# Moving the w_out sums on VectorE: behind the last square of chunk 0 instead of behind the second batch's K transpose

## The chip, the cores and the metric

The kernel runs on one core of one Trainium2 chip. The metric is the device time of one execution in microseconds (us). A profile of one execution comes with each kernel; its time axis starts at the first instruction, and its span is about 1.8 us shorter than the device time. The traced execution of a kernel is one of its timed runs, and every run has its mean granted TensorE clock beside its time (1.000 is full speed), so one can see whether a trace is typical.

## The reference, cut to what matters

```python
# attention with projected keys and values (8 batches, 8 heads, 1024 tokens, head size 64), then a feed-forward
k_proj = einsum('ks,bhsd->bhkd', E, k); v_proj = einsum('ks,bhsd->bhkd', F, v)
attn = softmax(q @ k_proj.T / sqrt(64));  x = attn @ v_proj        # x: 8192 x 512
h = maximum(x @ w_in, 0.0)                                         # w_in: 512 x 2048
out = (h * h) @ w_out                                              # w_out: 2048 x 512
```

## The kernel before

TensorE is the engine to keep busy. Each batch is cut into two chunks of 512 tokens. For a chunk, the first layer makes 16 blocks; ScalarE takes the relu of each and VectorE squares it. The second layer is then done in one of two ways. Chunk 0 of batch 0 uses plain products (L481). All later chunks use seven half-size products instead of eight, Strassen's scheme (L414), which needs sums of parts of `w_out` (`w_sum`, computed once) and of the squares (`h_sum`, computed per chunk).

```python
def sum_w_out(behind):
    with tc.issue_after(behind.queued.ins):     # these come later on VectorE than that instruction
        sum_w_out_now()

def sum_w_out_now():
    for j in range(2):
        ...
        up, down = w_out_sb[j], w_out_sb[j + 2]     # w_out arrives in four pieces
        b11, b12, b21, b22 = ...
        for o, x, y in ((t1, b12, b11), (t3, b22, b12), (t2, b22, t1), (t4, b21, t2)):
            nc.vector.tensor_tensor(out=o, in0=x, in1=y, op=ALU.subtract)      # L150, eight in all
```

The attention of the next chunk or batch is put between the steps of the feed-forward. `at(n, f)` traces `f` after step `n`. For batch 0, steps 1 to 16 are the first layer of chunk 0, 17 to 32 its second layer, 33 to 48 the first layer of chunk 1, and 49 on its seven products:

```python
at(21, att.transpose_q_chunk, 1, Q0, 0); at(21, att.transpose_q_chunk, 1, Q0, 1)  # PE, then VectorE copies qT (L269)
at(23, att.chunk_scores, 1, 0);          at(23, att.chunk_scores, 1, 1)           # PE, needs qT; ScalarE exp
at(25, att.sums, 0)                      # softmax sums: PE, three ScalarE passes, four VectorE copies of rs (L334)
at(27, att.chunk_values, 1, 0); ...      # values: PE, VectorE multiplies into xT (L375), which chunk 1 reads
...
at(39, nxt.transpose_k)                  # second batch; the old anchor of sum_w_out
at(45, nxt.sums, 0)
at(48, nxt.values, 0, True)              # True: its PSUM comes from the four banks that the products also use
at(46, sum_w_out, nxt)
```

Only TensorE's order is given by hand. On the other engines the scheduler chooses the order at compile time. In the profile lines, `ps_bank` and `ps_att` are the banks of PSUM, the memory that the matmuls of this kernel write; here a product can start only when one of its banks has been read out.

The softmax here doesn't subtract the row's maximum and nothing guards it: scores larger than these inputs give would overflow.

Of the kernel before, what the change touches and what calls it, by code (L numbers as in the profile page):

```python
# [12 lines left out]
ALU = mybir.AluOpType  # L13
# [5 lines left out]
def kernel(  # L19
# [11 lines left out]
    nc = tc.nc  # L31
# [21 lines left out]
    HF, HM = NFB // 2, DM // 2  # L53
# [19 lines left out]
    def bank(shape=(P, 512), dtype=F32):  # L73
        return fps.tile(list(shape), dtype, tag="bank", name="ps_bank")
# [91 lines left out]
    def projection(name, e_bf):  # L166
        ps = bank([P, NI, KP], BF16)
        view = e_bf[:].rearrange("k (p i) -> k i p", i=NI)
        for i in range(NI):
            nc.tensor.transpose(ps[:, i, :], view[:, i, :], ident[0:KP, 0:KP])  # L170
        t = const_pool.tile([P, NI, KP], BF16, name=name)
        nc.vector.tensor_copy(t[:], ps[:])
        return t

    def warm(n):

        ps = bank()
        for _ in range(n):
            nc.tensor.matmul(ps[:], lhsT=zeros[:, 0:P], rhs=zeros[:], start=True, stop=True)  # L179
# [5 lines left out]
    class Attention:  # L185
# [58 lines left out]
        def transpose_k(self, gs=(0, 1)):  # L244
            ps = bank([P, H // 2, 2, KP], BF16)
            rows = slice((LO, HI)[gs[0]].start, (LO, HI)[gs[-1]].stop)
            g = slice(gs[0], gs[-1] + 1)
            for j in range(H // 2):
                nc.tensor.transpose(
                    ps[:, j, g, :].rearrange("p g k -> p (g k)"),  # L250
                    self.kp[rows, j].rearrange("k a d -> k (a d)"), ident[rows, rows]
                )
            self.queued = nc.vector.tensor_copy(self.kT[:, :, g], ps[:, :, g])

        def transpose_k_dma(self):
            nc.sync.dma_start_transpose(
# [122 lines left out]
    class Ffn:  # L379
# [6 lines left out]
        def square(self, c, fb, ps):  # L386
            r = relu_pool.tile([P, TCH], BF16, name="h_relu")
            nc.scalar.activation(r[:], ps[:], AF.Relu)  # L388
            rv = r.rearrange("p (a t) -> p a t", a=2)
            nc.vector.tensor_tensor(out=self.hsq[c][:, fb // HF, :, fb % HF, :], in0=rv, in1=rv, op=ALU.mult)  # L390

        def quarter(self, c, kh, a):
            return self.hsq[c][:, kh, a]
# [153 lines left out]
    with tc.manual_schedule(engines={PE}):  # L547
        e_bf = soft_pool.tile([KP, S], BF16, tag="expT", name="e_bf")
        nc.vector.tensor_copy(e_bf[:], e_f32[:])
        nc.scalar.copy(K0[:, 0:2], k_f32[:])  # L550
        warm(8)
        ET = projection("ET", e_bf)
        warm(4)
        att = Attention(0)
        att.project_k(0)
        warm(1)
        att.transpose_q_chunk(0, Q0, 0)
        att.transpose_k((0,))
        warm(3)
        att.chunk_scores(0, 0)  # L560
        FT = projection("FT", f_bf)
        warm(3)
        att.project_k(1)
        att.chunk_sums(0, 0)
        att.transpose_q_chunk(0, Q0, 1)
        att.transpose_k((1,))
        warm(2)
        att.chunk_scores(0, 1)
        warm(2)
        att.project_v(V_PIECES[0])  # L570
        warm(1)
        att.chunk_sums(0, 1)
        att.chunk_values(0, 0)
        warm(2)

        coming = None
        for b in range(B):
            plan = {}

            def at(step, fn, *args, **kwargs):  # L580
                plan.setdefault(step, []).append(lambda: fn(*args, **kwargs))

            if b == 0:
                at(1, att.project_v, V_PIECES[1])
                at(2, att.chunk_values, 0, 1, (0,))
                at(2, att.project_v, V_PIECES[2])
                at(3, att.chunk_values, 0, 1, (1,))
                at(21, att.transpose_q_chunk, 1, Q0, 0)
                at(21, att.transpose_q_chunk, 1, Q0, 1)
                at(23, att.chunk_scores, 1, 0)  # L590
                at(23, att.chunk_scores, 1, 1)
                at(25, att.sums, 0)
                at(27, att.chunk_values, 1, 0)
                at(27, att.chunk_values, 1, 1)
                nxt = Attention(1)
                nxt.load()
            if b + 1 < B:
                if b + 2 < B:
                    coming = Attention(b + 2)
                    coming.load()  # L600
                if b == 0:
                    at(36, nxt.project)
                    at(39, nxt.transpose_q, 0)
                    at(39, nxt.transpose_q, 1)
                    at(39, nxt.transpose_k)
                    at(41, nxt.scores, 0)
                    at(41, nxt.scores, 1)
                    at(44, nxt.transpose_q, 2)
                    at(44, nxt.transpose_q, 3)
                    at(45, nxt.sums, 0)  # L610
                    at(48, nxt.values, 0, True)
                    at(48, nxt.scores, 2)
                    at(46, sum_w_out, nxt)
                    at(51, nxt.values, 1)
                    at(51, nxt.scores, 3)
                    at(55, nxt.sums, 2)
                    at(55, nxt.values, 2)
                    at(57, nxt.values, 3)
                else:
                    at(12, nxt.scores, 0)  # L620
                    at(12, nxt.scores, 1)
                    at(16, nxt.sums, 0)
                    at(16, nxt.values, 0)
                    at(20, nxt.scores, 2)
                    at(26, nxt.values, 1)
                    at(26, nxt.scores, 3)
                    at(46, nxt.sums, 2)
                    at(46, nxt.values, 2)
                    at(50, nxt.values, 3)
                if b + 2 < B:  # L630
                    if b == 0:
                        at(59, coming.project)
                        at(61, coming.transpose_q_dma)
                        at(62, coming.transpose_k)
                    else:
                        at(26, coming.project)
                        at(30, coming.transpose_q_dma)
                        at(28, coming.transpose_k_dma)
            for step, _ in enumerate(Ffn(att, b == 0).steps(), 1):
                for stage in plan.pop(step, []):  # L640
                    stage()
            assert not plan, plan
            att, nxt = nxt, coming
# [30 lines left out]
```

## Time and profile before

| | before |
|---|---|
| time, median of the first three runs | 499.49 us (498.38 to 499.56) |
| TensorE busy | 97% of the span |
| largest wait of TensorE after 30 us | 3.65 us, at 75.0 us |
| clock after it | 0.50 for 3.4 us |
| VectorE idle ahead of the chunk-1 softmax | 3.71 us and 5.95 us |

The page of the profile, kernel before (part 1: busy us, share of the span, instructions):

```profile
PE 482.8 (97%) x3446; PEld 293.4 (59%) x3482; DVE 310.9 (62%) x596; ACT 281.6 (57%) x426; POOL 32.5 (7%) x45
```

The timeline of TensorE, kernel before. The columns are start us, length us, engine, line, operation, output<-inputs, shape, count, and in brackets the idle time before it and what ended it:

```profile
37.53 4.48 PE L481 MATMUL ps_bank<-w_out,hsq 128*128 128x512 bf16 x20
...
42.74 1.89 PE L481 MATMUL ps_bank<-w_out,hsq 128*128 128x512 bf16 x8
...
54.19 3.87 PE L475 MATMUL ps_bank<-xT,w_in 128*128 128x512 bf16 x16
...
74.07 0.94 PE L414 MATMUL ps_bank<-w_out,hsq 128*128 128x256 bf16 x7
78.65 1.67 PE L414 MATMUL ps_bank<-w_out,hsq 128*128 128x256 bf16 x9 [3.65 <-DVE hsq L390]
...
96.95 10.52 PE L475 MATMUL ps_bank<-xT,w_in 128*128 128x512 bf16 x47
```

The reader should see one hole, at 75.0 us: the first of the seven products waits for a square (L390). The *start* is the first second-layer matmul of chunk 0 (37.53). **Stretch A** runs from the start to the first first-layer matmul of chunk 1 (54.19): 16.66 us. **Stretch B** runs from there to the first first-layer matmul of the third batch (96.95): 42.76 us.

The reason why the square is late is in the timeline of VectorE, kernel before:

```profile
42.49 1.29 DVE L269 COPY qT<-ps_bank 128x1024 bf16<-128x1024 bf16 x2 [3.71 <-PE ps_bank L265]
49.73 2.80 DVE L334 COPY rs<-rs 32x1024 f32<-32x1024 f32 x4 [5.95 <-ACT rs L329]
...
74.06 0.68 DVE L150 TENSOR_TENSOR w_sum<-w_out,w_out 128x1024 bf16<-128x1024 bf16 x1
74.75 2.78 DVE L334 COPY rs<-rs 32x1024 f32<-32x1024 f32 x4
77.56 0.69 DVE L150 TENSOR_TENSOR w_sum<-w_out,w_sum 128x1024 bf16<-128x1024 bf16 x1
78.17 0.42 DVE L390 TENSOR_TENSOR hsq<-h_relu 128x512 bf16<-128x512 bf16 x1
```

VectorE has no gap over 0.2 us from 59.98 to 84 us. The square's relu was done at 74.0 us, but two w_sum subtractions and four copies stand before it. Earlier, VectorE was idle for 3.71 and 5.95 us.

The clock, by narrow windows of the same trace (stretch, its length, busy us of TensorE, its weight loads, VectorE, ScalarE and GpSimd, then the granted TensorE clock; the last two columns, on DMA, are not used here):

```profile
78.00:79.00 1.00, 0.35 (x4) 0.32 (x5) 1.00 (x3) 0.00 (x0) 0.00 (x0) 1.00 1.25 209
79.50:80.00 0.50, 0.50 (x4) 0.37 (x3) 0.50 (x2) 0.00 (x0) 0.00 (x0) 0.50 1.24 205
83.00:84.00 1.00, 1.00 (x11) 0.90 (x10) 1.00 (x3) 0.94 (x1) 0.00 (x0) 1.00 1.25 209
```

### The profile page before, as it was taken

To read this page: it belongs to the slowest core of one execution; us is meant where nothing else is said; L and a number is where in the kernel's file an instruction comes from. 1 tells how busy PE (TensorE), PEld (TensorE's weight loads), DVE (VectorE), ACT (ScalarE), POOL (GpSimd) and SP (SyncE) were. 2 spreads that over 40 slices of the span, in tenths; PEclk is the share of its full clock that TensorE was granted. 3 is DMA by queue.
4 is the path that set the end of the run, shared out by engine and by line. 5 is a ranking of instruction groups with operands and counts; after the bars stand their busy time and mean duration, and the time that the engine had idled before them with its cause. 6 is when DMAs were issued, how large, how long until landed. Compare 5 with 4: busy or idle time off the path is not lost.

```text
span 497.8 us, 8559 instructions
## 1 busy us (share of the span) xinstructions
PE 482.8 (97%) x3446; PEld 293.4 (59%) x3482; DVE 310.9 (62%) x596; ACT 281.6 (57%) x426; POOL 32.5 (7%) x45
## 2 busy tenths in 40 slices
PE   7899997999999999999999999999999999999996
PEld 3444454647566574847557475665648475666755
DVE  2351797767584766757585675838566674847271
ACT  2464473476564846567573856558474665645451
POOL 7430100100100010000100000000000000000000
PEclk8999998999999999999999999999999999999999
DMA  9999999995992069710994016020611102020202
GB/s 172 204 205 213 237 208 207 218 179 113 201 196 85 1 120 196 144 59 1 190 212 119 0 53 129 3 84 1 123 58 47 40 2 85 1 86 0 86 1 86
DMA packets 75416, 54.30 MB, mean 109 GB/s; under 512 B 29168, under 2 KB 74480, under 8 KB 75376
## 3 DMA queue, kind: packets, MB, share of 16 engines
q0 software_dynamic: 30640, 29.23, 36.2%
q1 hardware_dynamic: 44736, 24.52, 19.6%
q8 instruction: 27, 0.44, 0.3%
q14 instruction: 13, 0.11, 0.1%
HBM read 59.24 MB, written 16.78 MB: 153 GB/s over the span
## 4 chain that ended last, share of the span: by engine, by line
PE 89%; DVE 6%; ACT 2%; issue 1%; DMA 1%; DVEq 0%; POOLq 0%
PE ps_bank L475 42%; PE ps_bank L414 37%; PE ps_bank L219 2%; PE ps_att L346 2%; PE ps_att L290 2%; DMA K_sb<-in_k_dram 1%; DVE rs L334 1%; PE ps_bank L481 1%; DVE xT L375 1%; PE ps_att L324 1%; DVE w_sum L150 1%; DVE hsq L390 1%; PE ps_bank L228 1%; PE ps_bank L179 1%; DVE qT L279 1%
## 5 line engine op out<-in xcount | busy, mean ns | idle before, releaser
L475 PE MATMUL ps_bank<-xT,w_in 128*128 128x512 bf16 x992 | 223.3, 379 | 3.0 <-DVE xT L375 1.1
L388 ACT ACTIVATE h_relu<-ps_bank 128x512 bf16<-128x512 f32 x256 | 151.1, 600 | 90.4 <-PE ps_bank L475 90.1
L475 PEld LDWEIGHTS <-w_in 128*128 128x128 bf16 x1024 | 99.2, 98 | 120.4 <-issue 6.2
L390 DVE TENSOR_TENSOR hsq<-h_relu 128x512 bf16<-128x512 bf16 x256 | 105.9, 423 | 84.3 <-ACT h_relu L388 83.0
L414 PEld LDWEIGHTS <-hsq 128*128 128x128 bf16 x960 | 92.1, 98 | 22.1 <-issue 6.9
L414 PEld LDWEIGHTS <-h_sum 128*128 128x128 bf16 x720 | 69.8, 98 | 12.4 <-issue 4.1
L414 PE MATMUL ps_bank<-w_out,hsq 128*128 128x256 bf16 x480 | 60.6, 274 | 3.6 <-DVE hsq L390 3.6
L414 PE MATMUL ps_bank<-w_sum,h_sum 128*128 128x256 bf16 x480 | 57.9, 275 | 0.0
L414 PE MATMUL ps_bank<-w_sum,hsq 128*128 128x256 bf16 x480 | 57.5, 272 | 0.3 <-ACT u L432 0.3
L424 DVE TENSOR_TENSOR o_sb<-ps_bank,u 128x512 f32<-128x512 f32 x30 | 20.7, 691 | 55.9 <-PE ps_bank L414 30.9
L334 DVE COPY rs<-rs 32x1024 f32<-32x1024 f32 x60 | 41.1, 685 | 11.7 <-ACT rs L329 10.6
L432 ACT COPY u<-ps_bank 128x512 f32<-128x512 f32 x30 | 17.5, 585 | 54.5 <-PE ps_bank L414 54.5
L304 ACT ACTIVATE expT<-ps_att 128x1024 bf16<-128x1024 f32 x32 | 31.9, 1025 | 6.6 <-PE ps_att L290 6.6
L350 DVE TENSOR_TENSOR xT<-ps_att,rs 128x512 bf16<-128x512 f32 x54 | 34.1, 685 | 0.4
L414 PE MATMUL ps_bank<-w_out,h_sum 128*128 128x256 bf16 x240 | 28.6, 273 | 0.5 <-DVE o_sb L424 0.5
L422 ACT COPY o_sb<-ps_bank 128x512 f32<-128x512 f32 x30 | 17.6, 585 | 17.7 <-PE ps_bank L414 17.6
L402 DVE TENSOR_TENSOR h_sum<-hsq 128x1024 bf16<-128x1024 bf16 x30 | 20.7, 691 | 1.0
L402 DVE TENSOR_TENSOR h_sum<-h_sum,hsq 128x1024 bf16<-128x1024 bf16 x30 | 20.6, 688 | 0.5
L402 DVE TENSOR_TENSOR hsq<-hsq 128x1024 bf16<-128x1024 bf16 x30 | 20.5, 685 | 0.0
L402 DVE TENSOR_TENSOR h_sum<-hsq,h_sum 128x1024 bf16<-128x1024 bf16 x30 | 20.5, 684 | 0.0
L80 POOL DMA_DIRECT2D K_sb<-in_k_dram x9 | 7.8, 861 | 138.5 <-PE ps_bank L220 134.1
L330 ACT ACTIVATE rs<-rs 128x1024 f32<-128x1024 f32 x15 | 15.9, 1062 | 0.5
(71 smaller groups left out, 251.0 us busy)
## 6 DMA issues: line engine op xcount, KB each, us to landing
out_dram<-o_sb SPq DMA_DIRECT2D x64, 256.0 KB, 2.3
K_sb<-in_k_dram POOLq DMA_DIRECT2D x7, 1024.0 KB, 13.7
V_sb<-in_v_dram POOLq DMA_DIRECT2D x7, 1024.0 KB, 19.7
Q_sb<-in_q_dram POOLq DMA_DIRECT2D x7, 1024.0 KB, 15.9
w_out<-in_moe_w_out_dram POOLq DMA_DIRECT2D x4, 512.0 KB, 17.8
w_in<-in_moe_w_in_dram POOLq DMA_DIRECT2D x3, 512.0 KB, 14.7
k_f<-in_k_dram SPq DMA_DIRECT2D x1, 512.0 KB, 4.3
Q_sb<-in_q_dram POOLq DMA_DIRECT2D x2, 256.0 KB, 8.1
```

The source lines that it names most:

```text
L304: nc.scalar.activation(e[:], ps[:], AF.Exp, scale=SCALE)
L330: nc.scalar.activation(rs[1][:], rs[1][:], AF.Exp, scale=-1.0)
L334: nc.vector.tensor_copy(rs[j][lack:lack + 32], rs[j][have:have + 32])
L350: nc.vector.tensor_tensor(out=self.xT[:, pr, :, par], in0=ps_x[par].rearrange("p (c t) -> p c t", c=2), in1=rs[:, par].rearrange("p (c t) ...
L388: nc.scalar.activation(r[:], ps[:], AF.Relu)
L390: nc.vector.tensor_tensor(out=self.hsq[c][:, fb // HF, :, fb % HF, :], in0=rv, in1=rv, op=ALU.mult)
L402: nc.vector.tensor_tensor(out=o, in0=x, in1=y, op=op)
L414: nc.tensor.matmul(ps[:, i * HM:(i + 1) * HM], lhsT=h[:, fb, i * P:(i + 1) * P], rhs=w_out_form(n, fb), start=fresh and i == 0 and fb == 0 ...
L422: nc.scalar.copy(o[:], ps[:])
L424: nc.vector.tensor_tensor(out=o[:], in0=ps[:], in1=more[:], op=ALU.add)
L432: nc.scalar.copy(u[:], ps[:])
L475: nc.tensor.matmul(ps[:], lhsT=w_in_blk(cb, fb), rhs=self.xT[:, cb, c].rearrange("p a t -> p (a t)"), start=(cb == 0), stop=(cb == NCB - 1),)
```

## The change

The intent is to take the eight subtractions (8 x 0.60 us = 4.8 us) out of the full stretch and put them into VectorE's idle time before chunk 1. The anchor becomes the last square of batch 0, chunk 0.

```diff
-            self.queued = nc.vector.tensor_copy(self.kT[:, :, g], ps[:, :, g])
+            nc.vector.tensor_copy(self.kT[:, :, g], ps[:, :, g])
 ...  # in Ffn.square
-            nc.vector.tensor_tensor(out=self.hsq[c][:, fb // HF, :, fb % HF, :], in0=rv, in1=rv, op=ALU.mult)
+            self.queued = nc.vector.tensor_tensor(out=self.hsq[c][:, fb // HF, :, fb % HF, :], in0=rv, in1=rv, op=ALU.mult)
 ...
             plan = {}
+            ffn = Ffn(att, b == 0)
 ...
-                    at(46, sum_w_out, nxt)
+                    at(18, sum_w_out, ffn)
 ...
-            for step, _ in enumerate(Ffn(att, b == 0).steps(), 1):
+            for step, _ in enumerate(ffn.steps(), 1):
```

## The prediction

> **What bounds the kernel.** By the page of the profile, TensorE is busy 97% of the 497.8 us span and carries 89% of the chain that ended last; VectorE is busy 62%. The exception is batch 0, chunk 1: the timeline shows VectorE back to back from 59.98 to about 84.3 us: squares, softmax copies, half sums and the eight w_sum subtractions (65.1 to 78.5 us, about 0.60 us each). The chain that ended last runs there through VectorE. TensorE's one large wait there is 3.65 us, 75.0 to 78.65 us, for the square of L390. In narrow windows the granted clock is 1.00 until 79, 0.50 from about 79.2 to 82.5, and 1.00 again; 17 second-layer matmuls take 3.40 us there, 16 elsewhere about 1.75. The Trainium skill ("TensorE: Matmul & The Clock Gate", Part 1) says the clock halves after an idle window of about 3.4 us and returns after a busy one; this trace agrees (3.3 us at half clock, 1.65 us lost). So the hole costs about 5.3 us.
>
> **What the change does.** No work is added. The eight subtractions, 8 x 0.6 = 4.8 us, may start behind the last square of chunk 0, which ends at 38.8 us; VectorE is then idle 3.7 us until 42.49 us and 5.95 us before 49.73 us. I expect them at about 38.8 to 43.7 us.
>
> Early cost: The qT copies (now 42.49 to 43.78) may slip by about 1.1 us. The chunk scores start at 44.56 us and their exponentials, held by ScalarE's store, at 45.15: mostly slack, 0 to 0.3 us lost. If the last w_out piece lands late (TensorE used it at 42.7 us without a wait), up to 0.8 us.
>
> Gain: replaying VectorE from 65.2 us without the sums, it keeps up with ScalarE until about 73.5 us. The square that TensorE waited for has its relu at 74.0 us and can end between 75.3 us (if ordered before the last two rs copies) and 76.8 us (after all four). Then the second product needs the first xT multiply (its PSUM bank) and the second half of the first h_sum, all after four copies and two squares: 73.55 + 4.7 = about 78.3 us. So the eight matmuls that ended at 81.98 us end at about 78.8 us, or near 77.5 in a kind order. No hole reaches 3.4 us, so the half clock goes: 3.2 to 4.5 us, kept to the end. Less the early cost: about 3.7 us, 0.7% of the time.
>
> **Predicted:** 495.8 us, range 494.0 to 498.2. Faster by over 2%: 0.01; within 2%: 0.985; slower: 0.005.
>
> **What would show it.** (1) w_sum at about 39 to 45 us, none after 60. (2) The 3.65 us wait for the square becomes 0.3 to 2 us. (3) The clock stays at 1.00 from 73 to 84 us. (4) A new wait of about 1 to 2 us where the second product starts, on xT or h_sum. (5) Chunk 1's first matmul (54.19) not over 0.5 us later; the third batch's first matmul (96.95) 3 to 4.5 us earlier, and that difference kept to the end.
>
> **What would make it wrong.** The scheduler reorders VectorE: sums placed ahead of qT with a wait for w_out, delaying chunk 1's softmax chain; or copies ahead of squares so that the hole stays near 3.4 us and the clock still drops (gain then about 1 to 2 us). Or a kinder order with hardly a hole: gain 5 us.

## The result, and the profile after

The changed kernel takes 497.38 us in the median (496.91 to 498.36, 4 runs); before took 498.94 us (498.32 to 499.56, 4 runs). The ratio is 0.9971, with an interval of 0.9949 to 0.9994. The gain is real but about 1.5 us, not the 3.7 us forecast, although the time lies inside the stated range.

The timeline of TensorE, kernel after:

```profile
35.78 4.48 PE L481 MATMUL ps_bank<-w_out,hsq 128*128 128x512 bf16 x20
...
42.31 1.02 PE L481 MATMUL ps_bank<-w_out,hsq 128*128 128x512 bf16 x4 [0.30 <-DMA w_out<-in_moe_w_out_dram]
44.24 0.41 PE L290 MATMUL ps_att<-qT,kT 64*64 64x256 bf16 x8 [0.91 <-DVE qT L269]
45.44 0.41 PE L290 MATMUL ps_att<-qT,kT 64*64 64x256 bf16 x8 [0.79 <-DVE qT L269]
45.78 3.14 PE L481 MATMUL ps_bank<-w_out,hsq 128*128 128x512 bf16 x8
...
56.26 3.77 PE L475 MATMUL ps_bank<-xT,w_in 128*128 128x512 bf16 x16
...
77.42 1.16 PE L414 MATMUL ps_bank<-w_out,hsq 128*128 128x256 bf16 x9 [0.45 <-DVE hsq L390]
79.88 1.21 PE L414 MATMUL ps_bank<-w_sum,h_sum 128*128 128x256 bf16 x8 [1.31 <-DVE xT L350]
...
95.74 10.52 PE L475 MATMUL ps_bank<-xT,w_in 128*128 128x512 bf16 x48
```

The hole for the square shrank from 3.65 to 0.45 us, and the new wait for xT (1.31 us) is where the prediction put it. Stretch B is 95.74 - 56.26 = 39.48 us. But stretch A is 56.26 - 35.78 = 20.48 us, against 16.66 before: TensorE now waits for qT twice, and the next eight matmuls take 3.14 us where eight took 1.89 before.

The timeline of VectorE, kernel after:

```profile
36.95 0.68 DVE L150 TENSOR_TENSOR w_sum<-w_out 128x1024 bf16<-128x1024 bf16 x1
...
39.36 0.68 DVE L150 TENSOR_TENSOR w_sum<-w_out,w_sum 128x1024 bf16<-128x1024 bf16 x1
42.29 0.69 DVE L150 TENSOR_TENSOR w_sum<-w_out,w_out 128x1024 bf16<-128x1024 bf16 x1 [2.25 <-DMA w_out<-in_moe_w_out_dram]
...
43.50 0.68 DVE L269 COPY qT<-ps_bank 128x1024 bf16<-128x1024 bf16 x1
44.11 0.68 DVE L150 TENSOR_TENSOR w_sum<-w_out,w_sum 128x1024 bf16<-128x1024 bf16 x1
44.70 0.68 DVE L269 COPY qT<-ps_bank 128x1024 bf16<-128x1024 bf16 x1
```

Five subtractions run at once. The sixth reads the fourth piece of w_out, which lands at 42.27 us, and VectorE stands still for 2.25 us with the qT copies behind it, though the transposes that they copy were done by 41.2 us. The Trainium skill ("TensorE: Matmul & The Clock Gate", Part 1, "Architectural detail") says that VectorE is a strict FIFO, and this trace agrees. The chain that ended last, kernel after, runs through exactly this (start us, length us, what):

```profile
22.10 20.17 DMA w_out<-in_moe_w_out_dram
...
42.29 1.29 DVE w_sum L150 x2
43.58 0.60 DVE qT L269
44.19 0.60 DVE w_sum L150
44.78 0.61 DVE qT L269
```

And the clock, by narrow windows of kernel after:

```profile
45.00:46.00 1.00, 0.56 (x9) 0.25 (x9) 0.38 (x1) 0.83 (x2) 0.00 (x0) 1.00 1.27 209
47.00:48.00 1.00, 1.00 (x4) 0.44 (x3) 0.00 (x0) 0.59 (x1) 0.00 (x0) 0.50 1.20 248
79.00:80.00 1.00, 0.12 (x2) 0.10 (x2) 1.00 (x3) 0.22 (x1) 0.00 (x0) 1.00 1.24 205
```

The half clock is gone at 79 us, as forecast, but for 3.4 us it has appeared at 46.3 to 49.7 us. Not in every run: this traced run took 498.36 us at a mean clock of 0.997, while the other three took 496.91 to 497.60 us at 0.999 to 1.000. The trace therefore shows about 1.5 us more loss than a typical run has. In the repeat (after_again, below) the one run with this fault is again the traced one; whether tracing favours it was not tested.

The first traces of the two kernels also differ by 1.75 us in the start (37.53 and 35.78). A second trace of the kernel before, below, has a start of 35.74, so that this is a difference between runs and no effect of the change; where it arises is shown there.

### The profile page after: what moved, and what is told of

The parts are those of the page before. It is cut to its first block, busy times and chain, and to the rows that moved or that the text cites. A ratio compares the mean times of both kernels' runs of the same rounds, so it can differ in the third digit from the quotient of the medians.

```text
span 496.6 us, 8595 instructions
## 1 busy us (share of the span) xinstructions
PE 484.8 (98%) x3482; PEld 292.1 (59%) x3482; DVE 311.3 (63%) x596; ACT 282.1 (57%) x426; POOL 32.5 (7%) x45
## 4 chain that ended last, share of the span: by engine, by line
PE 87%; DMA 7%; DVE 2%; POOL 1%; ACT 1%; issue 1%; POOLq 0%; DVEq 0%
PE ps_bank L475 41%; PE ps_bank L414 37%; DMA w_out<-in_moe_w_out_dram 4%; DMA V_sb<-in_v_dram 3%; PE ps_bank L219 2%; PE ps_bank L481 2%; PE ps_att L346 2%; PE ps_att L290 2%; PE ps_att L324 1%; DVE rs L334 1%; DVE xT L350 0%; ACT rs L329 0%; ACT rs L328 0%; DVE w_sum L150 0%; PE ps_bank L275 0%
## 5 line engine op out<-in xcount | busy, mean ns | idle before, releaser
L475 PE MATMUL ps_bank<-xT,w_in 128*128 128x512 bf16 x1024 | 226.6, 379 | 1.2 <-DVE xT L375 1.1
L475 PEld LDWEIGHTS <-w_in 128*128 128x128 bf16 x1024 | 99.2, 98 | 120.5 <-issue 6.0
L414 PEld LDWEIGHTS <-hsq 128*128 128x128 bf16 x960 | 91.9, 98 | 18.7 <-issue 6.9
L414 PEld LDWEIGHTS <-h_sum 128*128 128x128 bf16 x720 | 69.3, 98 | 13.4 <-issue 5.3
L414 PE MATMUL ps_bank<-w_out,hsq 128*128 128x256 bf16 x480 | 60.1, 273 | 0.4 <-DVE hsq L390 0.4
L414 PE MATMUL ps_bank<-w_sum,h_sum 128*128 128x256 bf16 x480 | 57.3, 273 | 1.3 <-DVE xT L350 1.3
L414 PE MATMUL ps_bank<-w_sum,hsq 128*128 128x256 bf16 x480 | 57.5, 273 | 0.3 <-ACT u L432 0.3
L414 PE MATMUL ps_bank<-w_out,h_sum 128*128 128x256 bf16 x240 | 28.6, 273 | 0.5 <-DVE o_sb L424 0.5
L402 DVE TENSOR_TENSOR hsq<-hsq 128x1024 bf16<-128x1024 bf16 x30 | 20.5, 684 | 0.0
L402 DVE TENSOR_TENSOR h_sum<-hsq,h_sum 128x1024 bf16<-128x1024 bf16 x30 | 20.5, 683 | 0.0
L328 ACT ACTIVATE rs<-ps_att 128x1024 f32<-128x1024 f32 x15 | 15.3, 1019 | 2.3 <-PE ps_att L324 2.3
```

The source lines that it names most:

```text
L328: nc.scalar.activation(rs[1][:], ps[:], AF.Ln)
L402: nc.vector.tensor_tensor(out=o, in0=x, in1=y, op=op)
L414: nc.tensor.matmul(ps[:, i * HM:(i + 1) * HM], lhsT=h[:, fb, i * P:(i + 1) * P], rhs=w_out_form(n, fb), start=fresh and i == 0 and fb == 0 ...
L475: nc.tensor.matmul(ps[:], lhsT=w_in_blk(cb, fb), rhs=self.xT[:, cb, c].rearrange("p a t -> p (a t)"), start=(cb == 0), stop=(cb == NCB - 1),)
```

## The experiments

The theory was: the late gain came as computed, and the loss is early, where the subtraction that needs the fourth w_out piece blocks VectorE with the qT copies behind it. The first rival was that 4.8 us of subtractions cost the chunk-1 softmax stage by themselves, wherever they stand in it. The marks read from the traces:

| kernel | start | A | B | clock of the traced run | ratio to before (interval) |
|---|---|---|---|---|---|
| before, first trace | 37.53 | 16.66 | 42.76 | 0.993 | |
| before_again | 35.74 | 17.12 | 43.84 | 0.992 | |
| after | 35.78 | 20.48 | 39.48 | 0.997 | 0.9971 (0.9949 to 0.9994) |
| after_again | 35.91 | 20.39 | 39.61 | 0.996 | 0.9960 (0.9943 to 0.9977) |
| behind_q | 35.98 | 16.97 | 39.59 | 1.000 | 0.9932 (0.9915 to 0.9948) |
| no_last_piece | 37.03 | 16.67 | 39.58 | 1.000 | 0.9932 (0.9918 to 0.9946) |
| keep_clock_early | 35.59 | 18.90 | 39.61 | 1.000 | 0.9959 (0.9937 to 0.9981) |
| keep_clock | 37.43 | 16.67 | 41.85 | 0.999 | 0.9980 (0.9966 to 0.9994) |
| half_early | 35.67 | 17.16 | 39.59 | 1.000 | 0.9928 (0.9907 to 0.9949) |
| sums_sooner | 39.46 | 16.67 | 38.95 | 0.993 | 0.9923 (0.9898 to 0.9948) |
| half_and_sooner | 35.68 | 17.19 | 39.71 | 1.000 | 0.9936 (0.9918 to 0.9955) |
| values_later | 37.03 | 16.67 | 43.03 | 0.997 | 0.9993 (0.9972 to 1.0013) |
| before_sooner | 36.92 | 16.66 | 42.78 | 0.997 | 1.0004 (0.9979 to 1.0028) |

### behind_q: the same subtractions behind the qT copies

```diff
-            nc.vector.tensor_copy(self.qT[:, 4 * hg:4 * hg + 4, 2 * c:2 * c + 2, :], ps[:])
+            self.q_copied = nc.vector.tensor_copy(self.qT[:, 4 * hg:4 * hg + 4, 2 * c:2 * c + 2, :], ps[:])
 ...
-        with tc.issue_after(behind.queued.ins):
+        with tc.issue_after(behind.q_copied.ins):
 ...
+                at(22, sum_w_out, att)      # and at(18, sum_w_out, ffn) is gone
```

> Same eight subtractions, queued behind the second qT copy of chunk 1 (so first-chunk idle time of VectorE after 44 us is used). Stretch A is from the first second-layer matmul of chunk 0 to the first first-layer matmul of chunk 1 (before 37.53 to 54.19 = 16.66 us, after 35.78 to 56.26 = 20.48 us); stretch B is from there to the first first-layer matmul of the third batch (before 42.76 us, after 39.48 us). Theory 1 (the loss is VectorE waiting in order for the last w_out piece with the qT copies behind it): A returns to 16.7 to 17.2 us, B stays 39.5 us, whole kernel 3 to 3.6 us under before, ratio 0.993 to 0.994. Rival (subtractions cost the chunk-1 softmax stage wherever they are put in it, by load on VectorE or its memory): A stays over 18 us, ratio 0.996 or more.

It took 495.79 us (494.99 to 496.18, 5 runs) beside 499.26 us, 3.5 us less. Set side by side up to 90 us, the two traces show that on VectorE only the two qT copies changed place against the changed kernel. The timeline of VectorE, behind_q:

```profile
40.94 1.29 DVE L269 COPY qT<-ps_bank 128x1024 bf16<-128x1024 bf16 x2 [3.71 <-PE ps_bank L265]
42.15 0.68 DVE L150 TENSOR_TENSOR w_sum<-w_out 128x1024 bf16<-128x1024 bf16 x1
...
45.75 1.42 DVE L150 TENSOR_TENSOR w_sum<-w_out,w_sum 128x1024 bf16<-128x1024 bf16 x2
48.49 2.80 DVE L334 COPY rs<-rs 32x1024 f32<-32x1024 f32 x4 [1.32 <-ACT rs L329]
```

All eight subtractions fit into the second idle stretch, and 1.32 us of it remain. A is 16.97 us. The rival falls: 4.8 us of subtractions in this stage cost nothing here, behind qT. Whether they may also stand in front of qT is the next question.

### no_last_piece: the changed order without the late load

```diff
-            up, down = w_out_sb[j], w_out_sb[j + 2]
+            up, down = w_out_sb[j], w_out_sb[2]      # wrong result on purpose
```

> The changed kernel, but the second half of the subtractions reads the third w_out piece in place of the fourth (wrong result on purpose), so the same work in the same order ahead of the qT copies with no late load to wait for. Theory 1 (the wait for the load is the loss): subtractions run without a gap from about 37 to 42 us, no wait of TensorE for qT over 0.3 us, A 16.7 to 17.2 us, B 39.5 us, ratio to before 0.993 to 0.994. Rival (4.8 us of work ahead of the qT copies is the loss by itself): A over 18 us, ratio 0.996 or more.

The result is wrong, as intended; the time is 495.86 us (495.09 to 496.16, 5 runs). VectorE's order is that of the changed kernel, but its timeline, no_last_piece, has no gap:

```profile
41.21 0.69 DVE L150 TENSOR_TENSOR w_sum<-w_out,w_out 128x1024 bf16<-128x1024 bf16 x1
41.81 0.69 DVE L150 TENSOR_TENSOR w_sum<-w_out,w_sum 128x1024 bf16<-128x1024 bf16 x1
42.41 0.69 DVE L269 COPY qT<-ps_bank 128x1024 bf16<-128x1024 bf16 x1
```

The start is 37.03 here, later than in the changed kernel's traces, so this trace alone is the easier case. But all five runs are within 495.1 to 496.2 us, at a clock of 1.000. So the loss is the wait for the fourth piece, not the work ahead of the copies. The four subtractions of half_early, below, stand ahead of qT in a trace with an early start (35.67 us), and A is 17.16 us there, so they cost nothing either.

### after_again and keep_clock_early: the half clock in the early stretch

after_again is the changed kernel unchanged.

> The changed kernel again, for its state of the clock and for comparison in the same rounds. Ratio to before 0.997; A between 18.5 us (clock kept) and 20.5 us (half clock for 3 us in it), B 39.5 us.

One run, the traced one, took 498.50 us at a clock of 0.996; the other four took 496.64 to 496.94 us at 0.999 to 1.000. In the same rounds behind_q took 495.79 us, so the block costs 1.1 us by the medians, and some 1.5 us more when the clock falls. keep_clock_early adds dummy matmuls where TensorE waits for qT:

```diff
         def chunk_scores(self, c, g):
             ps = att_psum()
+            for _ in range(3 if c == 1 else 0):
+                nc.tensor.matmul(ps[:, 0], lhsT=zeros[:, 0:P], rhs=zeros[:], start=True, stop=True)
```

> The changed kernel, with three dummy matmuls on zeros (0.65 us) ahead of each of the two score groups of chunk 1, where TensorE waits 0.91 and 0.79 us for qT. The waits for VectorE stay; only TensorE looks busier in them. If the 3 us at half clock seen at 46 to 49 us comes from those short holes together: the clock stays at 1.00 in the trace, A (first second-layer matmul of chunk 0 to first first-layer matmul of chunk 1) falls from 20.4 us to about 19 us, the slow runs of about 498.4 us go, ratio to before 0.995 to 0.996. If the half clock has another cause: A stays 20.4 us in the traced run and ratio 0.996 to 0.997.

Its six runs took 496.70 to 497.70 us, all at 0.999 or 1.000, and A in the trace fell from 20.4 to 18.90 us. This supports, but with one trace does not prove, that the short holes together brought the clock down. The mean hardly moves (0.9959 against 0.9960), as is to be expected where only one run in four or five had the fault. Six runs without a slow one are weak evidence by themselves; the 1.5 us in A is the better part.

### keep_clock: what the half clock cost the kernel before

```diff
             half = self.half_product
+            if self.cold:
+                for _ in range(13):      # 2.8 us of dummies on the bank that the first product then restarts
+                    nc.tensor.matmul(first[:], lhsT=zeros[:, 0:P], rhs=zeros[:], start=True, stop=True)
```

> The kernel before, with 13 dummy matmuls on zeros (2.8 us) put where TensorE waits 3.65 us for the square. The wait for VectorE is unchanged, only the clock should stay at 1.00. If the half clock after the hole costs time by itself: B falls from 42.76 us by 1.1 to 1.7 us, to 41.1 to 41.7 us, ratio 0.997. If the slow matmuls after the hole only follow VectorE's pace: B stays within 0.4 us of 42.76 us, ratio 0.999 to 1.001.

B fell by 0.91 us to 41.85, between the two forecasts, and the time fell to 0.9980. The half clock costs by itself, but less than the 1.65 us that I had taken: with the clock kept, TensorE meets a wait of 0.38 us for xT that the slow clock had covered. That is about half of the difference of 0.74 us; the rest was not traced to a cause. The timeline of TensorE, keep_clock (the added lines shift L475 and L481 by three; L414 stays):

```profile
78.56 1.16 PE L414 MATMUL ps_bank<-w_out,hsq 128*128 128x256 bf16 x9 [0.84 <-DVE hsq L390]
80.09 1.21 PE L414 MATMUL ps_bank<-w_sum,h_sum 128*128 128x256 bf16 x8 [0.38 <-DVE xT L350]
```

### before_again: how much the traces of one kernel differ

> The kernel before, for a second trace: A 16.7 to 17.2 us and B 42.7 to 42.8 us whatever the time at which chunk 0's second layer starts (37.5 us in the first trace; 35.6 to 37.5 us, once 39.5 us, in the others). Time about 499 us.

The time was 499.31 us and A 17.12 us, but B was 43.84 us, 1.1 us more than expected. The wait for the square is again 3.65 us. The clock differs: in the windows of this trace it is 0.75 between 76.0 and 76.5 us and 0.50 until 83 us, 6.8 us at half rate against 3.4 us in the first trace. The expectation missed that the same hole may cost one or two such spells: every half-rate spell on record in these traces lasts 3.41 us or 6.83 us. In the first trace the clock fell twice, at 7.46 and 79.14 us, and the 71.68 us between are 21 times 3.41 us, as if the changes lie on a fixed grid. Where a hole lies on it may decide whether the clock falls and for how long; no run here tests this. The timeline of TensorE, before_again:

```profile
35.74 4.48 PE L481 MATMUL ps_bank<-w_out,hsq 128*128 128x512 bf16 x20
42.27 1.02 PE L481 MATMUL ps_bank<-w_out,hsq 128*128 128x512 bf16 x4 [0.29 <-DMA w_out<-in_moe_w_out_dram]
...
52.86 3.87 PE L475 MATMUL ps_bank<-xT,w_in 128*128 128x512 bf16 x16
...
77.33 2.10 PE L414 MATMUL ps_bank<-w_out,hsq 128*128 128x256 bf16 x9 [3.65 <-DVE hsq L390]
```

This trace has the same start as the changed kernel's, so the two can be set side by side. A grew by 20.48 - 17.12 = 3.36 us, B fell by 43.84 - 39.48 = 4.36 us: net 1.0 us, and the two traced runs differ by 499.31 - 498.36 = 0.95 us. In a run whose clock holds early, another 1.5 us is kept.

The second line of the fence also shows that TensorE itself waits for the fourth piece when the start is early. In the first trace, the matmuls at 42.74 us that I had read as its first use were four of the third piece and then four of the fourth.

Where the start varies can be read from the kept traces. TensorE, kernel before and then before_again:

```profile
7.84 1.89 PE L228 MATMUL ps_bank<-K_sb,ET 128*64 128x256 bf16 x8 [0.99 <-DMA K_sb<-in_k_dram]
...
6.97 1.06 PE L228 MATMUL ps_bank<-K_sb,ET 128*64 128x256 bf16 x8
```

The first eight matmuls on K took 1.87 to 1.92 us in all six traces with a start of 36.9 us or later, and 1.03 to 1.06 us in all seven with a start of 36.0 us or earlier. In two of the six (before and sums_sooner) TensorE had waited 0.99 and 1.99 us for K and the clock is on record at 0.50 (3.41 and 6.83 us); with the late spell of before added, this also explains their mean clock of 0.993. In the other four the matmuls are as slow but the record shows 1.00 there, so that their cause is not shown.

### half_early and before_sooner: volume or order in the late stretch

half_early moves only the four subtractions of the first half, which do not read the fourth piece:

```diff
+                    at(18, sum_w_out, ffn, (0,))      # js: which halves
+                    at(46, sum_w_out, nxt, (1,))      # behind the K transpose, as before
```

> Only the four subtractions of the first half (they read the first and third w_out pieces) behind the last square of chunk 0; the other four behind the K transpose of the second batch, as before. Theory 1 (the late piece blocks VectorE): nothing waits for the last piece early, A is 16.7 to 17.0 us as before. If gain late grows with the work taken away: 2.4 us of the 4.8 us leave the late stretch, its hole falls under 3.4 us, the clock stays, B 40 to 41 us (before 42.76, all eight moved 39.5), ratio 0.994 to 0.996.

It took 495.72 us (495.01 to 496.34, 6 runs), and B is 39.59 us, as with all eight moved. So the gain does not grow with the work taken away: once 2.4 us are gone, VectorE has caught up by the time of the rs copies, and the scheduler puts the late square between the copies instead of behind all four. The timeline of VectorE, half_early:

```profile
72.20 1.38 DVE L334 COPY rs<-rs 32x1024 f32<-32x1024 f32 x2
73.62 0.43 DVE L390 TENSOR_TENSOR hsq<-h_relu 128x512 bf16<-128x512 bf16 x1
74.07 1.38 DVE L334 COPY rs<-rs 32x1024 f32<-32x1024 f32 x2
```

before_sooner is the kernel before with `at(44, nxt.sums, 0)` in place of 45, which brings the copies forward and leaves the volume:

> The kernel before with only the softmax sums one step earlier, all eight subtractions still late. If the late hole is a matter of VectorE's volume (4.8 us of subtractions ahead of the last square): the work ahead of the square is the same, hole 3 to 3.7 us, B 42 to 42.8 us, ratio 0.997 to 1.001. If it is mainly a matter of order (four copies ahead of the square): hole 1 to 2.2 us, clock kept, B 40 to 41 us, ratio 0.994 to 0.996.

It took 499.12 us (498.94 to 499.34, 4 runs). The hole was 3.17 us, B 42.78 us and the ratio 1.0004, so bringing the copies forward is no cure while the volume stays.

### values_later, sums_sooner, half_and_sooner: the remaining late waits

All three start from behind_q or half_early. values_later replaces `at(48, nxt.values, 0, True)` by `at(50, nxt.values, 0)`.

> All eight subtractions behind the second qT copy, and the first value product of the second batch two steps later and in an attention bank, so the second Strassen product no longer waits for its multiply to free a bank. Theory: of the two late waits (0.45 us for a square, 1.31 us for xT) the second falls to about 0.3 us, B 38.4 to 38.8 us instead of 39.5 us, ratio to before 0.991. Rival: another wait takes its place (the half sum h_sum, or the value product itself), B stays 39.3 us or more, ratio 0.993.

The rival was right, and worse: B rose to 43.03 us, and the time is 498.94 us (498.49 to 499.33, 6 runs), no gain over before. The timeline of TensorE, values_later:

```profile
80.56 0.41 PE L290 MATMUL ps_att<-qT,kT 64*64 64x512 bf16 x4 [2.05 <-DVE xT L350]
```

The wait for a bank moved to the attention tiles, where the next scores now wait 2.05 us, and the clock fell to 0.50 after it. sums_sooner is behind_q with `at(44, nxt.sums, 0)`:

> All eight subtractions behind the second qT copy, and the first softmax sums of the second batch one step earlier, so that VectorE's four rs copies come before the last squares instead of between them. Theory: the 0.45 us wait for the square goes and the 1.31 us wait for xT falls to under 0.6 us, B 38.2 to 38.8 us instead of 39.5 us, ratio to before 0.990 to 0.991. Rival: ScalarE, full from 72 to 75 us, delays the relus instead, B stays 39.3 us or more, ratio 0.993.

B is 38.95 us, 0.64 us less than behind_q and just short of the forecast, and the time is 495.25 us (494.53 to 497.67, 6 runs). The traced run is the slowest of the six: its 6.83 us at half clock lie before 15 us, outside both stretches. In the same rounds half_early took 495.72 us; the intervals of the two overlap, so it is not shown to be faster. half_and_sooner is half_early with the same edit:

> Candidate for the best version: four subtractions early (as half_early) and the first softmax sums of the second batch one step earlier (as sums_sooner). If the two changes add: A 16.7 to 17.2 us, B 38.9 us as in sums_sooner, ratio to before 0.991 to 0.993. If the four late subtractions and the earlier copies collide on VectorE: B 39.5 us or more, ratio 0.993 to 0.995.

B is 39.71 us and the time 495.81 us: the two changes do not add. TensorE waited 1.65 us for the square.

behind_q, half_early and sums_sooner beat the kernel before by 3.5 to 3.9 us by the medians of their rounds (499.26 or 499.18 us). behind_q also beat the changed kernel in the same rounds (495.79 against 496.92 us); the other two did not run beside it, but their ratios to before, 0.9928 and 0.9923, are below its 0.9971 and 0.9960. Which of the three is best is left open.

## Why the prediction was wrong

**Right: what bound the kernel and what the late side would give.** The prediction had "3.2 to 4.5 us". B fell by 3.28 us between the first two traces and by 4.36 us between the two with the same start. The wait for the square fell to 0.45 us (forecast 0.3 to 2), the clock stayed at 1.00 there, and the new wait of 1.31 us came on xT. behind_q, which has the late gain without the early loss, came out 3.5 us under before, inside these 3.2 to 4.5 us.

**Wrong: the early cost.** The step that failed was "mostly slack, 0 to 0.3 us lost. If the last w_out piece lands late ..., up to 0.8 us". It measured 3.36 us in the traces with one start, 1.5 us of it the half clock, and 1.1 us by medians against behind_q in the same rounds; the starts of the untraced runs are not on record. The prediction's own check (5), chunk 1's first matmul not over 0.5 us later, failed too: it moved from 54.19 to 56.26 us, although the start was 1.75 us earlier. "Sums placed ahead of qT with a wait for w_out" stood in the prediction's last paragraph as a risk, but with no size in the sum. Three things made it larger:

- The landing was misread. The DMA view of before gave 20.1 us at most from issue to landing for a w_out piece, and the last was issued at 22.56 us: 42.7 us. I took an unwaited use at 42.7 us as a bound instead, but those matmuls began with the third piece.
- The start was taken from one trace. The fourth piece landed between 42.1 and 42.7 us in every trace where it can be read off, while the starts seen are 35.6 to 39.5 us. By that difference, a run with a start of 35.8 us has 1.7 us more to wait than the one with 37.5 us that I planned from. For that one start "up to 0.8" was about right: by the forecast's own times the sixth subtraction would come at 38.8 + 5 x 0.6 = 41.8 us and wait 0.9 us for a landing at 42.7 us (an estimate).
- The clock was only considered for the one hole. With waits of 0.30 to 0.35, 0.91 and 0.79 us within 3.5 us it fell to half for 3.4 us in the two traced runs of this kernel.

**Partly mis-sized: the hole "costs about 5.3 us".** The half clock costs 0.91 us of B in keep_clock's pair of traces, not 1.65, in part because a wait of 0.38 us for xT lay hidden in it; in before_again it lasts twice as long.

**Missed by the replay: half would have done.** The replay took away all 4.8 us and did not ask how much was needed. half_early shows that 2.4 us give the same B.

What stays open is why in some runs K comes late and the first matmuls run at half speed, which together move the start by up to 3.9 us, and why the early half clock appears in some runs of the changed kernel and not in others.

## What to carry to other kernels

Before work is moved into an idle stretch of an in-order engine, list the arrival of every operand of every moved instruction, and put the ones with a late load behind whatever the critical engine needs next. Work whose operands are there may stand ahead of it, as long as it ends in time. Where a load's landing is fixed and the compute's phase is not, take the earliest phase seen, and give the risk that you can name a size in the sum. Test whether a part of the move is enough: here four of the eight subtractions, those that needed no late data, gave the whole gain.

## What the Trainium skill lacked or had wrong

- "TensorE: Matmul & The Clock Gate", Part 1: it names one idle window of about 3.4 us for the fall to half rate, and tells of frequent short idle times in one kernel without their size. Here the clock fell at the end of a hole of 3.17 us (before_sooner), 0.7 us after one of 2.05 us that followed shorter waits (values_later), and in two runs during or after three waits of 0.30 to 0.35, 0.91 and 0.79 us within 3.5 us. It stayed at 1.00 after 0.45 and 1.31 us (after, late stretch) and after 0.41 and 1.65 us (half_and_sooner).
- The same part says that the clock returns after at least one busy window of about 3.4 us. The lengths agree (3.41 or 6.83 us at half rate), but it does not say that the same hole can cost one window or two: after the 3.65 us hole it was one in the first trace of the kernel before, and two in before_again, where the clock fell 1.1 us before the hole ended.
- No page was found that gives the time from issue to landing of a load that is queued with others: 512 KB of w_out took 15.3 to 20.5 us here, with the DMA engines moving about 205 GB/s.
